# Threshold attention and a gated feed-forward layer on one core: the switch from the first to the second order of the work at slot 20 instead of slot 22

## The chip, the cores and the metric

The kernel runs on one core of one Trainium2 chip. The metric is the device time of one execution in microseconds (us). Engines are named as in the profile: PE (TensorE, matrix products and transposes), DVE (VectorE), ACT (ScalarE), POOL (GpSimd) and SP (SyncE, which here only issues DMAs). "PEld" is the loading of weights into PE.

## What is computed

Eight batches with eight heads, 576 tokens, head size 64. First an attention that keeps only scores near the row's maximum:

```python
scores = scale * np.matmul(q, k.transpose(0, 1, 3, 2))
thresh = np.max(scores, axis=-1, keepdims=True) - tau
scores = np.where(scores >= thresh, scores, -1000000000.0)
attn = softmax(scores)               # with 1e-09 added to the sum
x = np.matmul(attn, v)               # heads side by side: 4608 tokens x 512
```

Then a feed-forward layer on these 4608 tokens, with `w_in` of 512x2048 and `w_out` of 2048x512:

```python
h = x @ w_in
g = h * np.clip(h + 3.0, 0.0, 6.0) / 6.0
out = g @ w_out
```

## The kernel before, in words

**Slots.** Heads are taken four at a time (a quad, two pairs of heads; two quads make a batch, 16 quads in all). A quad has nine slots: four blocks of 128 query rows for each of its two pairs, and one slot (slot 8 of the quad) with the last 64 rows of all four heads. The 144 slots are walked by one hand-written loop. The program is not scheduled by a planner: each engine executes its instructions in the order in which the loop body emits them.

**One slot.** A slot `n` has these steps, for two heads at once:

- `scores` (L278): PE multiplies keys and queries in f32 into PSUM, 576 columns for each head.
- `sm_max` (L303): DVE copies the scores to SBUF and takes each row's maximum. `sm_bias` (L308): POOL makes the threshold from it.
- `sm_mask` (L312) and `sm_exp` (L317): ACT masks, then takes exponentials and their row sums.
- `sm_recip` (L320): DVE inverts the sums. `sm_norm` (L325): POOL scales the probabilities and writes them as bf16 (tile `pn`, four buffers).
- The probabilities are transposed for the product with the values. In most slots SP issues a DMA transpose (L333). In slots marked `on_chip` (L479: numbers below N1 - 1, in six of the nine places of a quad) PE does it with nine 128x128 transposes (L340) and DVE copies the result (L341).

**What stands beside the slots.** `av_main` and `av_rest` (L349, L352) multiply probabilities and values; `products` says after which slot. `turns` says in which slot a quad's queries and keys are transposed; in the first two batches PE does this (L233, L258, L260) and the results are copied out of PSUM by DVE, or, for the keys, by `copy_out` (L219), which picks DVE up to slot N1 and ACT afterwards.

**The feed-forward layer** is cut into items. One item of the first projection (`mm1`, L384) is eight 128x128 by 256 matmuls; ACT (even slots, L392) or DVE (odd slots, L394) computes relu(h + 3), and DVE multiplies it with h (`mm1_gate`, L407). An item's PSUM bank (HB) can be reused when its gate is done. The second projection (`mm2_part`, L418) is cut into parts of four 128x128 by 512 matmuls; four parts make a tile of 128 tokens, which DVE or ACT scales (L426, L424) and SP writes out (L439).
 
**Two orders.** Up to slot N1 - 1 the loop runs the first order: scores for slot n + 2 in every slot, exponentials one slot late, no feed-forward work. From slot N1 on it runs the second order: one first-projection item in each slot as long as `todo1` has one, two parts of the second projection (`second`, L520, `pieces`) in each even slot as long as `todo2` has some, and scores for the next two slots in one burst at the end of each odd slot. In the second order the scores of odd slots lie in other PSUM columns (`first`, L272) than those of even slots. If `pieces` is not zero, the item of the following odd slot cannot use bank OB, which holds the second projection's sum, and goes to HB. Up to slot N2 (28) ACT takes the exponentials of an even slot ahead of its relu, later behind it.

**DMAs.** SP loads queries and keys; POOL loads values, both weight matrices (with a cast to bf16, one or two pieces in a slot, the last pieces of `w_out` in slots 28 and 29) and, from quad 4 on, the last 64 rows of the keys (`rest`, L124).

**The end.** Behind the loop, `rest1` and `rest2` work off the remaining items. The last token tile is one sum of sixteen matmuls; `last_out` (L656) has ACT scale and write its left half and DVE its right half.

Of the kernel before, what the change touches and what calls it, by code (L numbers as in the profile page):

```python
# [9 lines left out]
F32 = mybir.dt.float32  # L10
# [3 lines left out]
Act = mybir.ActivationFunctionType  # L14

P = 128
# [4 lines left out]
def kernel(  # L21
# [10 lines left out]
    nc = tc.nc  # L32
    B, H, S, D = q.shape
    assert (B, H, S, D) == (8, 8, 576, 64)
    d_model, d_ff = moe_w_in.shape
    NPAIR = H // 2
    KI = d_model // P
    NI = d_ff // P
    NQUAD = B * H // 4
    NSLOT = 9  # L40
    NB = 2
    N0 = 3
    N1 = 22
    N2 = 28
    HB, OB = 6, 7
    scale = 1.0 / math.sqrt(D)
# [14 lines left out]
    o_pool = ctx.enter_context(tc.tile_pool(name="op", bufs=3))  # L61
# [5 lines left out]
    ps = ps_pool.tile([P, 8, 512], F32, name="ps")  # L67
# [15 lines left out]
    def load_quad(quad):  # L83
        b, g = divmod(quad, 2)
        nat[quad] = (nat_pool.tile([P, 1152], F32, tag="nq", name="nq"),
                     nat_pool.tile([P, 4, 4, D], F32, tag="km", name="km"),
                     nat_pool.tile([P, 2 * D], F32, tag="kr", name="kr"))
        nq, km, kr = nat[quad]

        def main(dst, src, h, order, by=nc.sync):  # L90
            by.dma_start(out=dst[:, :, h, :], in_=src[b, 4 * g + h, 0:512, :].rearrange(order, t=4))

        def blocks_q(n, a, j):
            c = 32 * (2 * a + j)
            nc.sync.dma_start(out=nq[c:c + 32, n * S:(n + 1) * S].rearrange("p (k d) -> p k d", d=32),
                              in_=q[b, 4 * g + 2 * n + a, :, 32 * j:32 * j + 32].rearrange("(k r) d -> r k d", r=32))

        def blocks_k(n, a, j):
            c = 32 * (2 * a + j)
            nc.sync.dma_start(  # L100
                out=km[c:c + 32].rearrange("p t h d -> p (t h d)")[:, n * 512:(n + 1) * 512].rearrange(
                    "p (t m d) -> p t m d", t=4, d=32),
                in_=k[b, 4 * g + 2 * n + a, 0:512, 32 * j:32 * j + 32].rearrange("(m r t) d -> r t m d", r=32, t=4))

        def load_k(n):
            if b < NB:
                for a in range(2):
                    main(km, k, 2 * n + a, "(p t) d -> p t d")
            else:
                for a in range(2):  # L110
                    for j in range(2):
                        blocks_k(n, a, j)

        def load_q(n):
            if b < NB:
                for a in range(2):
                    main(nq[:, 0:1024].rearrange("p (t h d) -> p t h d", h=4, t=4), q, 2 * n + a, "(t p) d -> p t d",
                         by=nc.scalar if quad == n == 0 else nc.sync)
            else:
                for a in range(2):  # L120
                    for j in range(2):
                        blocks_q(n, a, j)

        def rest():  # L124
            for dst, src in ((kr[:], k), (nq[:, 1024:1152], q))[0:2 if b < NB else 1]:
                for n in range(2):
                    (nc.sync if b < NB else nc.gpsimd).dma_start(out=dst[64 * n:64 * n + 64, :].rearrange("p (h d) -> p h d", h=2),
                                      in_=src[b, 4 * g + 2 * n:4 * g + 2 * n + 2, 512:S, :].rearrange("h p d -> p h d"))

        def both():  # L130
            rest()
            load_k(1)

        if b < NB:
            loads.extend((lambda: load_k(0), lambda: load_q(0), rest, lambda: load_k(1), lambda: load_q(1)))
        else:
            loads.extend((lambda: load_q(0), lambda: load_k(0), lambda: load_q(1), both))
# [22 lines left out]
    w_out_sb = singles.tile([P, NI, d_model], BF16)  # L160
# [34 lines left out]
    gbuf = g_pool.tile([P, NI, 2 * S], BF16, name="g")  # L195
# [21 lines left out]


    def copy_out(out, in_):  # L219
        if 0 <= now <= N1:  # L220
            nc.vector.tensor_copy(out=out, in_=in_)
        else:
            nc.scalar.copy(out=out, in_=in_)  # L223
# [46 lines left out]
        return evict  # L270

    def first(n):  # L272
        return n > N1 + 2 and n % 2

    def score_col(n, a):
        return (704 if first(n) else 128) + (0 if a else 1536)
# [137 lines left out]
    def mm2_part(bb, mt, part, ob=OB):  # L414
        if part == 0:
            o_ps[0] = ps[:, ob, :]
        for ni in range(part * 4, part * 4 + 4):
            nc.tensor.matmul(o_ps[0], gbuf[:, ni, mt * P:(mt + 1) * P], w_out_sb[:, ni, :],  # L418
                             start=(ni == 0), stop=(ni == NI - 1))
# [17 lines left out]
    def flush():  # L437
        for o, i in late:
            nc.sync.dma_start(out=i, in_=o)  # L439
        late.clear()  # L440
# [34 lines left out]
    for quad in range(NQUAD):  # L475
        for slot in range(NSLOT):
            sl = Slot()
            sl.quad, sl.slot, sl.n = quad, slot, len(queue)
            sl.on_chip = len(queue) < N1 - 1 and (slot in (1, 3, 5, 7, 8) or slot == 0 and quad > 0)  # L479
            queue.append(sl)  # L480
    scores(0)
    sm_max(queue[0])
    sm_bias(queue[0])
    scores(1)

    turns = {1: [("q", 1)], 2: [("k", 1)], 3: [("rest", 0)]}

    def turn_at(n, job, of):
        turns.setdefault(n, []).append((job, of))
# [10 lines left out]
    for quad in range(NQUAD):  # L500
        p0, p1 = 2 * quad, 2 * quad + 1
        if quad < NB:
            jobs = ((8, p0, 0, 512), (13 - 2 * quad, p1, 0, 512), (15 - 3 * quad, None, 0, 0))
        else:
            jobs = [(7 - quad % 2 + 2 * i, *of) for i, of in enumerate(
                ((p0, 0, 256), (p0, 256, 256), (p1, 0, 256), (p1, 256, 256), (None, 0, 0)))]
        for after, *of in jobs:
            products.setdefault(quad * NSLOT + after, []).append((quad, *of))
# [10 lines left out]

    def second():  # L520
        nonlocal pieces, bb, mt, part
        pieces = 2 if now % 2 == 0 and todo2 else 0
        for _ in range(pieces):
            bb, mt, part = todo2.pop(0)
            mm2_part(bb, mt, part)
# [127 lines left out]
    count = [1, 0 if todo2 and todo2[0][2] else 1]  # L653


    def last_out():  # L656
        osb = o_pool.tile([P, d_model], F32, tag="osb", name="osb")
        r0, c = B * S - 64 - P, d_model // 2
        nc.scalar.activation(out=osb[:, 0:c], in_=o_ps[0][:, 0:c], func=Act.Copy, scale=1.0 / 6.0)
        nc.scalar.dma_start(out=out[r0:r0 + P, 0:c], in_=osb[:, 0:c])  # L660
        nc.vector.tensor_scalar_mul(out=osb[:, c:2 * c], in0=o_ps[0][:, c:2 * c], scalar1=1.0 / 6.0)
        nc.sync.dma_start(out=out[r0:r0 + P, c:2 * c], in_=osb[:, c:2 * c])

    def rest1(item, then, on_act=True):
        h = mm1(item, hb=(0, 1, 3, 4)[count[0] % 4])
# [4 lines left out]
    def rest2():  # L670
        while todo2:
            bb, mt, part = todo2.pop(0)
            mm2_part(bb, mt, part, ob=OB - count[1] % 2)
            if part == 3:
                flush()
                if (bb, mt) == (B // 2 - 1, 8):
                    last_out()
                else:
                    late.extend(mm2_out(bb, mt, on_act=(count[1] % 2 == 0)))
                count[1] += 1  # L680

    av_main(2 * last + 1, 0, 256)()
# [50 lines left out]
```

## Time and profile before

| what | us |
|---|---|
| median of 7 runs (lowest to highest) | 516.6 (516.39 to 517.53) |
| the profiled execution | 516.39 |
| span of its trace | 514.6 |
| PE busy | 504.2 (98%) |
| ACT busy | 451.8 (88%) |
| DVE busy | 441.9 (86%) |
| POOL busy | 300.0 (58%) |

So 1.8 us of the profiled execution lie outside the span. The granted TensorE clock is 0.998 of full speed. "Busy" is to be read with care: the ends of pipelined matmuls are modelled, so PE counts as busy for part of the time in which it waits. Which engine sets the pace of a stage is read from the chain of waits and from the timeline, not from the shares alone.

### The profile page before, as it was taken

The numbers are of one execution on the slowest core, as the hardware profiler recorded it, in microseconds if no ns is written. First come the engines' busy times: TensorE is split into PE (matmuls) and PEld (weight loads), VectorE is DVE, ScalarE is ACT, GpSimd is POOL, SyncE is SP. The second block draws the span as 40 slices with busy tenths as digits, with TensorE's granted clock in tenths as the row PEclk, the third lists the DMA queues.
The fourth block names the chain that finished last, engine by engine and source line by source line (L and its number), as shares of the span: only waits on it lengthen the run. The fifth ranks groups of instructions, "written<-read, shape, count | busy, mean of one in ns | idle before, by whom it ended". The sixth has DMA issues, their size and how long they took to land.

```text
span 514.6 us, 12094 instructions
## 1 busy us (share of the span) xinstructions
PE 504.2 (98%) x4127; PEld 318.1 (62%) x4127; DVE 441.9 (86%) x1124; ACT 451.8 (88%) x980; POOL 300.0 (58%) x538
## 2 busy tenths in 40 slices
PE   8999999999999999999999999999999999999997
PEld 6655566666656666666656666666655666667563
DVE  3789898998999999999999999999999999887260
ACT  3999989999999999999999999999999999986060
POOL 1788888756666666666566756667566655552000
PEclk9999999999999999999999999999999999999999
DMA  6998999989999999999899999999999996655132
GB/s 140 176 165 144 155 149 173 166 150 193 163 167 162 177 178 150 181 170 171 162 182 152 187 165 164 169 159 175 156 172 174 182 177 115 113 103 89 74 63 61
DMA packets 314094, 78.77 MB, mean 153 GB/s; under 512 B 296624, under 2 KB 309168, under 8 KB 314032
## 3 DMA queue, kind: packets, MB, share of 16 engines
q1 hardware_dynamic: 294464, 67.90, 77.5%
q0 software_dynamic: 18368, 9.71, 15.3%
q8 instruction: 32, 0.52, 0.4%
q10 hardware_dynamic: 1200, 0.39, 0.3%
q14 instruction: 30, 0.25, 0.2%
HBM read 36.70 MB, written 9.44 MB: 90 GB/s over the span
## 4 chain that ended last, share of the span: by engine, by line
PE 79%; ACT 5%; DVE 2%; issue 0%
PE ps L288 24%; PE ps L418 24%; PE ps L384 20%; PE ps L349 7%; PE ps L379 3%; ACT s L317 2%; ACT s L312 2%; PE ps L352 1%; ACT r L392 1%; DVE g L407 1%; DVE r L394 0%; PE ps L340 0%; DVE s L303 0%; ACT kT L223 0%; PE ps L258 0%
## 5 line engine op out<-in xcount | busy, mean ns | idle before, releaser
L325 POOL TENSOR_SCALAR pn<-s,rinv 128x576 bf16<-128x576 f32 x288 | 211.4, 747 | 18.9 <-issue 4.8
L303 DVE TENSOR_SCALAR_CACHE_REDUCE s<-ps 128x576 f32<-128x576 f32 x288 | 205.0, 748 | 16.5 <-PE ps L288 8.3
L312 ACT ACTIVATE s<-s,bias 128x576 f32<-128x576 f32 x288 | 205.8, 763 | 5.1 <-POOL bias L308 4.7
L317 ACT ACTIVATE s<-s 128x576 f32<-128x576 f32 x288 | 192.5, 671 | 0.3
L288 PE MATMUL ps<-kT,qT 64*128 64x384 f32 (+7 forms) x1280 | 175.4, 419 | 3.9 <-DVE s L303 2.4
L288 PEld LDWEIGHTS ps<-kT,qT 64*128 64x128 f32 (+1 forms) x1280 | 102.9, 175 | 60.3 <-issue 15.8
L418 PE MATMUL ps<-w_out_sb,g 128*128 128x512 bf16 x576 | 134.1, 379 | 0.0
L384 PE MATMUL ps<-xT,w_in_sb 128*128 128x256 bf16 x1024 | 130.9, 273 | 0.8 <-DVE g L407 0.8
L384 PEld LDWEIGHTS <-w_in_sb 128*128 128x128 bf16 x1024 | 95.7, 98 | 40.6 <-issue 21.7
L308 POOL TENSOR_SCALAR bias<-m 128x2 f32<-128x2 f32 x144 | 27.1, 188 | 150.5 <-DVE rinv L320 133.8
L407 DVE SCALAR_TENSOR_TENSOR g<-r,ps 128x512 bf16<-128x512 f32 x128 | 87.8, 686 | 14.9 <-ACT r L392 11.0
L418 PEld LDWEIGHTS <-g 128*128 128x128 bf16 x576 | 56.2, 98 | 56.8 <-issue 0.4
L392 ACT ACTIVATE r<-ps,three 128x512 f32<-128x512 f32 x81 | 55.6, 687 | 24.7 <-PE ps L384 20.4
L317 ACT ACTIVATION_READ_ACCUMULATOR s<-s 128x1 f32 x288 | 54.6, 189 | 0.0
L394 DVE TENSOR_SCALAR r<-ps 128x512 f32<-128x512 f32 x63 | 42.8, 680 | 0.0
L349 PE MATMUL ps<-pT,vm 128*64 128x256 bf16 (+1 forms) x480 | 39.1, 285 | 0.0
L349 PEld LDWEIGHTS <-vm 128*64 128x64 bf16 x736 | 27.2, 110 | 16.1 <-issue 14.4
L360 DVE CAST xT<-ps 128x256 bf16<-128x256 f32 (+1 forms) x60 | 26.2, 436 | 10.2 <-PE ps L352 10.2
L426 DVE TENSOR_SCALAR osb<-ps 128x512 f32<-128x512 f32 x31 | 20.8, 673 | 8.4 <-PE ps L418 8.4
L303 DVE DVE_READ_ACCUMULATOR s<-ps 128x1 f32 x288 | 23.8, 83 | 0.0
L320 DVE RECIPROCAL rinv<-rsum 128x2 f32<-128x2 f32 x144 | 23.0, 160 | 0.6 <-ACT s L317 0.6
L144 POOL DMA_DIRECT2D vm<-in_v_dram x28 | 21.4, 766 | 0.7 <-issue 0.7
(57 smaller groups left out, 252.4 us busy)
## 6 DMA issues: line engine op xcount, KB each, us to landing
out_dram<-osb SPq DMA_DIRECT2D x31, 256.0 KB, 2.6
nq<-in_q_dram SPq DMA_DIRECT2D x96, 72.0 KB, 3.4
km<-in_k_dram SPq DMA_DIRECT2D x96, 64.0 KB, 3.2
vm<-in_v_dram POOLq DMA_DIRECT2D x24, 128.0 KB, 3.9
km<-in_k_dram SPq DMA_DIRECT2D x16, 128.0 KB, 3.8
w_in_sb<-in_moe_w_in_dram POOLq DMA_DIRECT2D x16, 128.0 KB, 3.7
w_out_sb<-in_moe_w_out_dram POOLq DMA_DIRECT2D x16, 128.0 KB, 3.7
pT<-pn SPq DMA_TRANSPOSE x117, 3.8
```

The source lines that it names most:

```text
L288: nc.tensor.matmul(ps_flat[rows, c0:c0 + w], qT_of(pair)[a * 64:(a + 1) * 64, q0:q0 + rows.stop - rows.start], kT_of(pair)[a * 64:(a + 1) ...
L303: nc.vector.tensor_scalar(out=sl.s[:, i, :], in0=ps_flat[:, c0:c0 + S], scalar1=1.0, scalar2=None, op0=Alu.mult, op1=Alu.max, accum_out=sl ...
L308: nc.gpsimd.tensor_scalar(out=sl.bias[:], in0=sl.m[:], scalar1=-scale, scalar2=tau, op0=Alu.mult, op1=Alu.add)
L312: nc.scalar.activation(out=s, in_=s, func=Act.Prelu, bias=sl.bias[:, i:i + 1], scale=scale, alpha=REJECT)
L317: nc.scalar.activation(out=s, in_=s, func=Act.Exp, accum_out=sl.rsum[:, i:i + 1])
L325: nc.gpsimd.tensor_scalar(out=pn[:, i, :], in0=sl.s[:, i, :], scalar1=sl.rinv[:, i:i + 1], scalar2=1.0, op0=Alu.mult, op1=Alu.mult)
L349: nc.tensor.matmul(pb[a * 64:(a + 1) * 64, :], vm[:, 2 * hp + a, c * D:(c + 1) * D], pT[:, 5 * a + c, cols], start=(c == 0), stop=False)
L384: nc.tensor.matmul(ps[:, hb, n * 256:(n + 1) * 256], w_in_sb[:, ki, (ni + n) * P:(ni + n + 1) * P], xT[b][:, ki, c0:c0 + 256], start=(ki = ...
L392: nc.scalar.activation(out=r, in_=hps, func=Act.Relu, bias=three[:])
L394: nc.vector.tensor_scalar(out=r, in0=hps, scalar1=3.0, scalar2=0.0, op0=Alu.add, op1=Alu.max)
L407: nc.vector.scalar_tensor_tensor(out=out, in0=r, scalar=6.0, in1=hps, op0=Alu.min, op1=Alu.mult)
L418: nc.tensor.matmul(o_ps[0], gbuf[:, ni, mt * P:(mt + 1) * P], w_out_sb[:, ni, :], start=(ni == 0), stop=(ni == NI - 1))
```

## The change

It has five parts.

1. `N1` is 20 instead of 22. The second order begins two slots earlier. With it, slots 17, 18 and 19 are no longer transposed by PE and DVE but by DMA (`N1 - 3` in place of `N1 - 1`), and `first` holds for slot 23 too.
2. The products of quad 1's second pair are taken in two column halves after slots 18 and 21, and its last rows after slot 23; before, the whole pair came after slot 20 and the last rows after slot 21. `second` gets a table: three parts in slot 36, one in each of slots 38, 42 and 44, otherwise two.
3. The last rows of quad 4's keys are loaded by SP instead of POOL.
4. `copy_out` uses DVE up to slot 23 (before: 22). The keys of pair 1 are transposed in slot 1 instead of slot 2.
5. The last token tile is multiplied in two column halves, in PSUM banks 2 and 5; DVE scales each, ACT's queue and SP write them.

```diff
-    N1 = 22
+    N1 = 20
...
-                    (nc.sync if b < NB else nc.gpsimd).dma_start(out=dst[64 * n:64 * n + 64, :].rearrange("p (h d) -> p h d", h=2),
+                    (nc.sync if quad < 5 else nc.gpsimd).dma_start(out=dst[64 * n:64 * n + 64, :].rearrange("p (h d) -> p h d", h=2),
...
     def copy_out(out, in_):
-        if 0 <= now <= N1:
+        if 0 <= now < N1 + 4:
...
     def first(n):
-        return n > N1 + 2 and n % 2
+        return n > N1 + 2 and n % 2 == 1
...
-            sl.on_chip = len(queue) < N1 - 1 and (slot in (1, 3, 5, 7, 8) or slot == 0 and quad > 0)
+            sl.on_chip = len(queue) < N1 - 3 and (slot in (1, 3, 5, 7, 8) or slot == 0 and quad > 0)
...
-    turns = {1: [("q", 1)], 2: [("k", 1)], 3: [("rest", 0)]}
+    turns = {1: [("q", 1), ("k", 1)], 3: [("rest", 0)]}
...
-            jobs = ((8, p0, 0, 512), (13 - 2 * quad, p1, 0, 512), (15 - 3 * quad, None, 0, 0))
+            jobs = (((8, p0, 0, 512), (9, p1, 0, 256), (12, p1, 256, 256), (14, None, 0, 0)) if quad else
+                    ((8, p0, 0, 512), (13, p1, 0, 512), (15, None, 0, 0)))
...
-        pieces = 2 if now % 2 == 0 and todo2 else 0
+        pieces = min(len(todo2), {36: 3, 38: 1, 42: 1, 44: 1}.get(now, 2)) if now % 2 == 0 else 0
...
-    def last_out():
-        osb = o_pool.tile([P, d_model], F32, tag="osb", name="osb")
+    def last_tile(mt):
         r0, c = B * S - 64 - P, d_model // 2
-        nc.scalar.activation(out=osb[:, 0:c], in_=o_ps[0][:, 0:c], func=Act.Copy, scale=1.0 / 6.0)
-        nc.scalar.dma_start(out=out[r0:r0 + P, 0:c], in_=osb[:, 0:c])
-        nc.vector.tensor_scalar_mul(out=osb[:, c:2 * c], in0=o_ps[0][:, c:2 * c], scalar1=1.0 / 6.0)
-        nc.sync.dma_start(out=out[r0:r0 + P, c:2 * c], in_=osb[:, c:2 * c])
+        for half, by in enumerate((nc.scalar, nc.sync)):
+            o_half, columns = ps[:, (2, 5)[half], 0:c], slice(half * c, half * c + c)
+            for ni in range(NI):
+                nc.tensor.matmul(o_half, gbuf[:, ni, mt * P:(mt + 1) * P], w_out_sb[:, ni, columns],
+                                 start=(ni == 0), stop=(ni == NI - 1))
+            osb = o_pool.tile([P, d_model], F32, tag="osb", name="osb")
+            nc.vector.tensor_scalar_mul(out=osb[:, 0:c], in0=o_half, scalar1=1.0 / 6.0)
+            by.dma_start(out=out[r0:r0 + P, columns], in_=osb[:, 0:c])
...
             bb, mt, part = todo2.pop(0)
+            if (bb, mt) == (B // 2 - 1, 8):
+                flush()
+                last_tile(mt)
+                todo2.clear()
+                continue
             mm2_part(bb, mt, part, ob=OB - count[1] % 2)
             if part == 3:
                 flush()
-                if (bb, mt) == (B // 2 - 1, 8):
-                    last_out()
-                else:
-                    late.extend(mm2_out(bb, mt, on_act=(count[1] % 2 == 0)))
+                late.extend(mm2_out(bb, mt, on_act=(count[1] % 2 == 0)))
```

## The prediction, as it was put on record

> **What bounds the kernel now.** I read the slices and the chain's shares first:
>
> ```profile
> PE   8999999999999999999999999999999999999997
> ...
> PE 79%; ACT 5%; DVE 2%; issue 0%
> ```
>
> PE is full in every slice, but ACT (88% of the span) and DVE (86%) nearly so, and the shares do not say which one sets the pace where. The chain of waits, in order of time, does:
>
> ```profile
> 90.16 1.34 ACT s L317 x4
> ...
> 110.99 0.98 PE ps L384 x8
> 111.97 1.73 PE ps L418 x8
> ```
>
> From 77.6 to about 104 us (slots 23 to 31) the chain runs through ACT's exponentials and masks; from about 106 us on it is PE alone, a pair of slots taking 6.38 to 6.5 us (first-projection item 0.98, two parts 1.73, item 0.98, values about 0.6, scores 2.14). So a slot moved ahead of 106 us competes with ACT and DVE, and work taken out behind it is worth PE time, down to what ACT needs for a pair: four exponentials and four masks at 0.67 and one relu of 0.69, 6.0.
>
> How full DVE is where the second order begins, I read from the busy time by stretches:
>
> ```profile
> core 0: us, PE busy (x) PEld busy (x) DVE busy (x) ACT busy (x) POOL busy (x), PEclk, DMA share, GB/s
> ...
> 66.43:92.72 26.29, 25.64 (x237) 17.23 (x234) 24.34 (x64) 24.46 (x55) 22.64 (x42) 1.00 1.04 162
> ```
>
> DVE idles 1.95 us and ACT 1.83 of 26.3. POOL's and PE's columns are no guide (PE's includes waiting).
>
> **What moves as a whole.** The order of the built instructions shows that behind slot 45 PE's sequence is the same in both kernels, the end included, but for the last tile. So no feed-forward work leaves the end: the items run out. The two items that move to slots 20 and 21 are missing from slots 36 and 37, and slot 28 gains two parts of the second projection and slot 36 one, taken from slots 38, 42 and 44, one from each. The account is therefore: what the early slots pay, against what slots 36 to 45 give back. PE's own work falls only by 27 transposes (9 take 0.55 from start to start of the next, 1.65 in all), in a stretch where PE is not the bound.
>
> **1. Keys of pair 1 in slot 1: -0.2.** In slot 2 PE waits 0.87 for DVE's copy of these keys (18.00 us), and ACT then 0.40 for a bias (21.13). With the copy (0.67) in slot 1 that wait goes, but four transposes (0.60) stand ahead of the scores of slot 3 and delay its mask by about 0.2. Ends: 0 to -0.4. The keys' DMA was issued by 6.1 us and lands 3.8 later by its group; it is needed at 14.
>
> **2. Slots 17 to 27.** On DVE three transposed copies (0.74) and a copy of 0.68 go: 2.9. Added are two gates (0.69), one relu (0.68), two half copies (0.42) and two key copies (0.28, from ACT): 3.5. DVE has 0.6 more to do, against 1.95 idle. On ACT a relu of 0.69 is added; two key copies (0.53) go, and two waits: 0.95 at 77.08 for the copy queued ahead on DVE, and 0.70 at 71.22, where the mask of slot 22 waits for a bias that POOL makes at 71.00, behind the issue of the last key rows (69.10 to 70.35) and of a weight piece. The kernel after takes that issue off POOL. So at slot 28 ACT is about 1.5 ahead by its own count and DVE 0.6 behind if none of its idle time is used. Each waits for the other, so I take 0.4 ahead: the maximum that starts at 91.40 (slot 29's) starts at 91.0. Ends: 0.6 behind, 1.5 ahead.
>
> SP's load: it gets three transposes (1.3 each) and two key loads (0.65 each), 5.2 us, behind blocks of four loads of 2.9 to 3.8. Counted on from 58.3, the transpose of slot 20 is issued at about 77.6 instead of 73.3 and, by its median landing of 3.8 (up to 5.6 in this stretch), lands at 82. The product that reads it is at 87.7 (slot 27), and the scaling that reuses its buffer at 83.6. It fits, with 1 to 2 us to spare. The product of slots 18 and 19 comes at 82 and its data at 77.
>
> **3. Slots 28 to 31: the new wait.** Slot 28 now has two parts, so slot 29's item goes to bank HB and waits for slot 28's gate. That gate is late, because up to slot 28 ACT's relu stands behind the exponentials:
>
> ```profile
> 90.84 1.92 PE L384 MATMUL ps<-xT,w_in_sb 128*128 128x256 bf16 x16
> ...
> 94.06 0.68 ACT L392 ACTIVATE r<-ps,three 128x512 f32<-128x512 f32 x1
> ...
> 94.77 0.69 DVE L407 SCALAR_TENSOR_TENSOR g<-r,ps 128x512 bf16<-128x512 f32 x1 [0.54 <-ACT r L392]
> ```
>
> Before, both items run in one go at 90.84, the parts of slot 30 first follow at 97.42, and the gate at 94.77 delays nobody. After: DVE does the maxima of slots 29 and 30 from 91.0 to 93.9, the gate to 94.55. PE, done with its parts at about 93.5, waits for it. Queued behind on PE are slot 29's item (to 95.6), the values (96.15), the scores of 32 and 31 (98.3), slot 30's item (99.25) and parts (101.0). DVE waits for these scores with the maximum of 31, ACT with slot 30's relu. On DVE: copy, relu, gate, key transpose (0.70), maximum to 100.0, gate of slot 30 to 100.8. PE goes on at 101.0: item, values 102.55, scores, and slot 32's item starts at 104.7. Before it starts at 103.85. **Cost of 2 and 3 together: +0.85.** Ends: +2.1 (DVE 0.6 behind, and gate and relu in series with the scores once more) and -1.0 (nothing waits).
>
> The last piece of `w_out` is issued by POOL at 97.20; the group's 3.7 puts it at 100.9. Slot 30's eighth matmul now reads it, at 99.25 + 7 x 0.216 = 100.8, so this wait is nothing as long as the one above stands; if the early slots go faster, it is what is late next.
>
> **4. Slots 36 to 45: -1.8.** Slots 36 and 37 lose two items (1.96) and gain a part (0.87): the pair of 6.49 becomes 5.40, above ACT's 5.33 without a relu: -1.09. In the pairs from 38, 42 and 44 a part of 0.87 goes, but it covers the way from item to gate:
>
> ```profile
> 343.95 1.05 PE L384 MATMUL ps<-xT,w_in_sb 128*128 128x256 bf16 x8
> ...
> 345.04 0.69 ACT L392 ACTIVATE r<-ps,three 128x512 f32<-128x512 f32 x1 [0.84 <-PE ps L384]
> ...
> 345.75 0.69 DVE L407 SCALAR_TENSOR_TENSOR g<-r,ps 128x512 bf16<-128x512 f32 x1
> ```
>
> The item ends at 344.93, the gate at 346.44, 1.51 later; the next item starts at 346.56. Two parts (1.73) fill that, one (0.87) leaves 0.64 of waiting. Each pair gains 0.23, three 0.69. Ends: -1.1 (the three give nothing) and -2.2 (they gain down to ACT's 6.0).
>
> **5. The last tile: -0.4.**
>
> ```profile
> 510.81 0.38 ACT L659 ACTIVATE osb<-ps 128x256 f32<-128x256 f32 x1 [2.86 <-PE ps L418]
> ...
> 511.23 0.42 DVE L661 TENSOR_SCALAR osb<-ps 128x256 f32<-128x256 f32 x1 [6.63 <-ACT osb L659]
> 511.68 0.34 SPq L662 DMA_DIRECT2D out_dram<-osb  x1
> ```
>
> DVE's half waits for ACT's half: from PE's end to the last issue 0.90. After, 0.04 + 0.42 + 0.03 remain: -0.41. The product in halves is 32 matmuls of 256 columns instead of 16 of 512: by the chain's rows 3.49 for 32 such (item rows at 491.70) against 10.37 / 48 x 16 = 3.46: +0.03. The last DMA is again 128 KB. Ends: -0.5 and, at the 0.122 of an isolated item's matmul (0.98 / 8), +0.03.
>
> Here a rule speaks against the change. The Trainium skill, page "TensorE: Matmul & The Clock Gate", section "Back-to-back issue gap", gives 81 ns for a sustained matmul of 128 columns with its weight load and 131 ns for one of 512, so that halving the columns would far from halve the time. An estimate from that page, 98 ns in between, makes the halves 3.13 against 2.10, and this step a loss of 0.6. The trace's 0.216 and 0.109 do not show such a floor at 256 columns, and I go by them.
>
> **Sum:** -0.2 + 0.85 - 1.78 - 0.38 = -1.51. Against the profiled execution (span 514.6 + 1.8 = 516.39): **514.9 us**. The median of the runs shown is 516.6, 0.2 higher.
>
> **Rivals.**
> A. The early slots come free: ACT is 1.5 ahead at slot 28 and most of the wait in 29 is absorbed. Then steps 2 and 3 cost between +0.2 and -1.0, and the time is 513.0 to 514.2. For it: DVE's 1.95 idle. Against it: the series of gate and scores above, and `w_out`'s last piece.
> B. The gain is used up: steps 2 and 3 cost 1.5 to 2.1, and at the upper end the thin pairs give only 1.1. That is -0.2 + 1.5 - 1.78 - 0.38 = -0.9 to -0.2 + 2.1 - 1.1 - 0.4 = +0.4, so 515.5 to 516.8. For it: DVE and PE then take turns. Against it: the idle time that DVE has now.
> C. Slower, by SP's queue: the DMA engines' share is 1.04 in 66 to 93 us. If the transpose of slot 20 lands later still than counted, POOL's scaling of slot 24 waits for its buffer, the maxima four slots on wait for theirs, and each further us goes into the time. With the slack of those buffers it decides from a landing behind about 85.5; at 89 it costs 3.5 against 1.5 won: 518.4. Landings of at most 5.6 speak against it.
>
> **How the numbers follow.** Forecast (514.2 to 515.5): 0.44. A: 0.24. B: 0.24. C: 0.08. The range leaves out C and the outer quarters of A and B, 0.2 in all: 513.3 to 516.4. About 0.2% (1.03 us) is what a measurement of this kernel can tell from no change. Faster by more are A and 0.40 of the forecast; within it are the other 0.04 and B; slower is C. So faster 0.64, within 0.2% 0.28, slower 0.08.
>
> **What would show it.** Right: in slot 29 PE's item waits for `DVE g L407` for about 1 us; slot 32's item starts 0.5 to 1 later than 103.85 (less 0.2); slot 46's about 1.1 earlier than 149.55; at the end no DVE wait for ACT, and the last issue about 0.5 us behind PE. Wrong: PE waiting for a DMA in slot 30 (`w_out`), POOL's scaling waiting for a DMA at 82 to 86 us, pairs of 6.4 in slots 38 to 45, or the last 32 matmuls taking over 3.6.

## The result, and the profile after

The kernel after takes 525.9 us (median of 16 runs, 519.09 to 529.37), the kernel before 516.65 (41 runs, 516.39 to 517.58). The ratio is 1.0138, 95% interval 1.0122 to 1.0153 (here and below ratios leave out the longest executions as disturbed, which the medians contain): **slower**, where 514.9 was predicted, and even the lowest time of after lies above each of these 41 times of before. The profiled execution of after is a long one, 529.37 (span 527.6); what it shows is compared below with shorter ones of its variants.

The page of after, with lines that answer to those of before (slices of PE, its granted clock, shares of the chain; last, the median landing of `w_out`'s pieces, that is the time from issue to arrival in us, 3.7 before):

```profile
PE   8999998669999999999999999999999999999997
...
PEclk9999999969999999999999999999999999999999
...
PE 78%; DMA 5%; DVE 3%; ACT 2%; POOL 1%; issue 0%; POOLq 0%; DVEq 0%
...
w_out_sb<-in_moe_w_out_dram POOLq DMA_DIRECT2D x16, 128.0 KB, 8.5
```

Nearly all of the loss lies in two slices of 13.2 us (92 to 119 us): from slot 28's first-projection item to slot 32's the trace takes 25.4 us, before 13.0, and the whole span is 13.0 longer. PE is no longer full there, its clock falls, and DMAs stand in the chain, where there were none. The chain of waits of after, in order of time (start, duration, what), names them:

```profile
79.69 6.04 DMA pT<-pn
...
85.91 0.76 POOL pn L325
...
90.06 11.77 DMA pT<-pn
...
102.00 1.41 POOL pn L325 x2
103.42 8.08 DMA w_out_sb<-in_moe_w_out_dram
...
112.34 1.71 PE ps L384 x8
...
117.97 0.98 PE ps L384 x8
```

The first link is slot 20's transpose: issued at 79.69, landed at 85.73, and POOL's scaling, which reuses its buffer, starts only then. Four slots later the same stands there again: slot 24's transpose takes 11.77, POOL's scaling of slot 28 waits for it until 102.00, and only behind that scaling does POOL issue the last piece of `w_out`. The last two lines are two items of the same size, 1.71 at 112 us and 0.98 at 118: it is the clock that differs.

So `w_out`'s last piece is late for two reasons. Its landing takes longer (8.08 against 3.6), and it is issued 6.2 us later than before, because POOL, which issues it, first has to wait for a buffer that a transpose still reads. POOL's timeline, after and then before:

```profile
102.00 1.47 POOL L325 TENSOR_SCALAR pn<-s,rinv 128x576 bf16<-128x576 f32 x2 [1.29 <-DMA pT<-pn]
103.42 0.58 POOL L169 DMA_DIRECT2D w_out_sb<-in_moe_w_out_dram  x1
```

```profile
97.20 0.57 POOL L169 DMA_DIRECT2D w_out_sb<-in_moe_w_out_dram  x1
```

The timeline of after for PE shows the predicted wait in slot 29 (first line) and then waits inside the second projection, of which two are printed:

```profile
96.94 1.03 PE L384 MATMUL ps<-xT,w_in_sb 128*128 128x256 bf16 x8 [1.68 <-DVE g L407]
...
105.98 0.46 PE L418 MATMUL ps<-w_out_sb,g 128*128 128x512 bf16 x1 [2.95 <-DMA w_out_sb<-in_moe_w_out_dram]
...
109.45 0.59 PE L418 MATMUL ps<-w_out_sb,g 128*128 128x512 bf16 x1 [1.70 <-DMA w_out_sb<-in_moe_w_out_dram]
```

They are four, 2.95, 0.73, 1.70 and 1.50: 6.9 us of waiting for single pieces of `w_out`, the last of which lands at 111.5 (before: 100.8). The busy time by stretches, after and then before (columns as in the prediction: busy us of PE, PEld, DVE, ACT, POOL, then the granted clock, the DMA engines' share, and GB/s):

```profile
84.00:90.00 6.00, 5.36 (x52) 3.78 (x48) 5.78 (x16) 6.00 (x14) 4.30 (x10) 1.00 1.28 141
...
102.00:108.00 6.00, 2.08 (x8) 0.59 (x6) 2.99 (x11) 3.64 (x8) 3.50 (x6) 0.85 1.36 113
108.00:114.00 6.00, 3.05 (x13) 1.49 (x12) 0.69 (x1) 1.59 (x5) 1.80 (x4) 0.50 1.23 198
```

```profile
84.00:90.00 6.00, 5.68 (x46) 3.83 (x46) 5.84 (x16) 6.00 (x14) 5.03 (x10) 1.00 1.13 184
```

In 84 to 90 us the DMA engines are busier than before (share 1.28 against 1.13) and move a quarter less, 141 against 184 GB/s. And in the last two stretches, 102 to 108 and 108 to 114 us, PE gets 0.85 and then 0.50 of its clock.

How the queue gets there can be read from the DMA part of both traces for 80 to 100 us (issues, KB each, median us to landing), before and then after:

```profile
w_out_sb<-in_moe_w_out_dram POOLq DMA_DIRECT2D x10, 128.0 KB, 3.7
pT<-pn SPq DMA_TRANSPOSE x6, 5.3
```

```profile
w_out_sb<-in_moe_w_out_dram POOLq DMA_DIRECT2D x11, 128.0 KB, 9.5
pT<-pn SPq DMA_TRANSPOSE x6, 10.6
```

The demand is the same, six transposes (and one of the last rows) and ten or eleven pieces, and landings take 2.0 and 2.6 times as long. In the trace of after the transposes issued at 79.69, 81.63, 83.28, 86.99, 90.06 and 93.26 land at 85.73, 89.51, 93.16, 98.27, 101.82 and 106.49, one in 3.5 to 5.1 us, while a slot wants one in about 3.0. The first three of them were issued within 3.6 us, because SP had come late out of two key-row loads and four key loads (75.52 to 79.59). In before, SP is through with its loads at 73.1; the three from slot 20 on are issued at 73.27, 75.15 and 78.81 and land in 4.0 to 5.9.

### The profile page after: what moved, and what is told of

Its sections match the earlier page's. It is cut to its first block, busy times and chain, and to the rows that moved or that the text cites. A ratio compares the mean times of both kernels' runs of the same rounds, so it can differ in the third digit from the quotient of the medians.

```text
span 527.6 us, 12086 instructions
## 1 busy us (share of the span) xinstructions
PE 507.0 (96%) x4126; PEld 320.6 (61%) x4126; DVE 441.5 (84%) x1125; ACT 451.4 (86%) x977; POOL 298.8 (57%) x536
## 4 chain that ended last, share of the span: by engine, by line
PE 78%; DMA 5%; DVE 3%; ACT 2%; POOL 1%; issue 0%; POOLq 0%; DVEq 0%
PE ps L288 24%; PE ps L418 22%; PE ps L384 20%; PE ps L349 7%; DMA pT<-pn 3%; PE ps L379 3%; DMA w_out_sb<-in_moe_w_out_dram 2%; PE ps L352 1%; DVE s L303 1%; DVE g L407 1%; ACT s L317 1%; PE ps L662 1%; ACT r L392 1%; ACT s L312 1%; POOL pn L325 1%; DVE r L394 0%
## 5 line engine op out<-in xcount | busy, mean ns | idle before, releaser
L288 PE MATMUL ps<-kT,qT 64*128 64x192 f32 (+7 forms) x1280 | 175.0, 420 | 2.3 <-DVE s L303 1.9
L418 PE MATMUL ps<-w_out_sb,g 128*128 128x512 bf16 x560 | 132.4, 380 | 6.9 <-DMA w_out_sb<-in_moe_w_out_dram 6.9
L418 PEld LDWEIGHTS <-g 128*128 128x128 bf16 x560 | 54.5, 98 | 61.5 <-issue 7.2
```

The lines of the kernel that those rows point to most:

```text
L288: nc.tensor.matmul(ps_flat[rows, c0:c0 + w], qT_of(pair)[a * 64:(a + 1) * 64, q0:q0 + rows.stop - rows.start], kT_of(pair)[a * 64:(a + 1) ...
```

## The experiments

Two theories stood against each other: that the loss is a **backlog of the DMA engines** (transposes and `w_out` pieces together) which the change tips over, and that the **order from slot 20** is itself the loss, whatever the DMAs do. All times were taken beside runs of the kernel before with medians of 516.7 to 516.9 (single times of before reach 519.4 in the set of e5 to e8, 518.0 in the others). "Landing" is the longest of a transpose issued in 66 to 112 us, and of a piece of `w_out`, in the profiled execution; "PE waits" is for DMAs, 60 to 140 us.

| run | us: median (lowest to highest) | ratio (95% interval) | landing, us | PE waits, us |
|---|---|---|---|---|
| before | 516.65 (516.39 to 517.58) | | 5.9 / 5.6 | 0 |
| after | 525.9 (519.09 to 529.37) | 1.0138 (1.0122 to 1.0153) | 13.2 / 11.8 | 7.2 |
| e1 | 525.83 (525.69 to 526.23) | 1.0176 (1.016 to 1.0191) | 5.8 / 5.9 | 0 |
| e13 | 518.42 (517.99 to 520.63) | 1.0033 (1.0018 to 1.0048) | 9.3 / 8.1 | 0 |
| e2 | 517.61 (516.24 to 520.74) | 1.0022 (1.0002 to 1.0041) | 8.2 / 6.9 | 0.6 |
| e10 | 516.88 (516.37 to 517.98) | 1.0004 (0.9995 to 1.0013) | 7.4 / 5.3 | 1.1 |
| e4 | 518.78 (517.18 to 525.4) | 1.0032 (1.0021 to 1.0042) | 10.0 / 8.0 | 3.4 |
| e6 | 518.64 (517.13 to 521.65) | 1.0026 (1.0009 to 1.0043) | 10.6 / 7.8 | 2.2 |
| e5 | 519.81 (517.41 to 527.47) | 1.0038 (1.0019 to 1.0057) | 7.8 / 6.9 | 0 |
| e12, e5 again | 522.09 (519.17 to 526.63) | 1.0107 (1.0057 to 1.0158) | 11.9 / 10.2 | 5.8 |
| e14 | 518.33 (517.0 to 519.36) | 1.0027 (1.0015 to 1.0038) | 7.1 / 6.4 | 0.9 |
| e3 | 520.65 (516.79 to 523.71) | 1.0067 (1.0036 to 1.0098) | 10.5 / 8.6 | 3.2 |
| e7 | 521.17 (520.4 to 522.49) | 1.0074 (1.0051 to 1.0098) | 11.2 / 9.5 | 4.5 |
| e9 | 524.36 (520.57 to 527.88) | 1.0142 (1.009 to 1.0195) | 12.8 / 10.8 | 7.4 |
| e8 | 515.59 (515.47 to 516.25) | 0.9969 (0.9958 to 0.9981) | 7.0 / 6.3 | 0 |
| e11 | 513.97 (513.83 to 515.01) | 0.9947 (0.9933 to 0.996) | 6.5 / 5.9 | 0 |
| e15 | 516.72 (514.51 to 517.71) | 0.9993 (0.9979 to 1.0008) | 7.2 / 5.8 | 1.6 |

### Taking the load off the queue: e1 and e13

e1 is after with slots 17 to 19 transposed by PE and DVE, as before:

```diff
-            sl.on_chip = len(queue) < N1 - 3 and (
+            sl.on_chip = len(queue) < N1 and (
```

> The kernel after, but slots 17, 18 and 19 are transposed by PE and DVE again, so that three DMA transposes go. Theory Q (queue): these three transposes fill the DMA queue ahead of the last pieces of w_out, so with them gone w_out lands about 4 us after its issue (kernel after: 8.5 in the median), PE waits for no DMA in slots 28 to 30, and the time falls to 514.5 to 517; the three transposes on PE and DVE cost up to 2 us of that. Theory N (early need): w_out is simply read two slots too early, and the queue is full anyway; then w_out lands about as late as in the kernel after, and the time stays above 519.

The landings are those of before again and no PE wait for a DMA is left, so the three transposes belong to the backlog. This is not shown cleanly, since e1 also issues the later transposes further apart (at 82.40, 87.19 and 91.24). The time did not fall to 514.5 to 517 as theory Q had it, for a reason of its own: these nine-fold transposes now stand in the second order. Waits of e1, 60 to 130 us (total, times, longest):

```profile
ACT r L392 <- PE ps L384: 12.1, 4, 8.9
...
PE ps L384 <- DVE pT L341: 3.2, 2, 2.4
```

ACT stands for 8.9 us in one piece behind an item that PE has behind the transposes. The run therefore says that these DMAs matter, and nothing on the price of the order. e13 does that: it loads only eight of `w_out`'s sixteen pieces and uses each twice (half of `w_out` is left out).

```diff
-        for ni in range(NI):
+        for ni in range(8):
...
-                             ... w_out_sb[:, ni, :],
+                             ... w_out_sb[:, ni % 8, :],
...
```

> The kernel after, but only the first eight of the sixteen pieces of w_out are loaded, and the second projection multiplies with each of them twice: half of w_out is left out of the computation, while every engine has the same instructions but for the eight DMAs that POOL no longer issues between slots 24 and 29. Theory Q (the loss is a backlog of the DMA engines between 80 and 112 us, and w_out's pieces are a part of that backlog as well as its first victims): no wait of PE for w_out, the transposes issued from 80 us on land in under 8 us instead of 9 to 13, the granted clock stays at 1.0, and what is left is the cost of the order at slot 20 without any wait, +0.5 to +1.0: 517.0 to 517.8. Theory W (the transposes are late by themselves, with or without w_out): they still land in 9 to 12 us, PE waits for pT instead, and the time is 519 to 523. Theory R (only the last pieces come too late for the second projection, the order itself is the gain that the prediction saw): 514.9 to 515.5.

518.42: no PE wait for a DMA, full clock, but landings up to 9.3, more than the backlog theory allowed. The DMA part of e13, again 80 to 100 us:

```profile
w_out_sb<-in_moe_w_out_dram POOLq DMA_DIRECT2D x4, 128.0 KB, 6.5
pT<-pn SPq DMA_TRANSPOSE x8, 5.7
```

The backlog builds up as in after (slot 22's transpose, issued at 83.24, lands at 92.50) and is gone as soon as the last piece, issued at 84.3, has landed at 92.4: the next transposes land at 93.38, 94.41 and 96.20, one in 0.9 to 1.8 us instead of one in 3.5 to 5.1. So the two kinds together are the load, and without the late pieces 7.5 of the 9.2 us between the medians are gone (by the ratios 5.4 of 7.1). What stays, 1.6, is put down to the order and some late transposes (POOL waits 2.2 for them).

### What tips the queue: e2, e10, e4, e6, e5, e12, e14

e2 adds the three DMA transposes to before; e10 adds the key rows by SP as well:

```diff
-            sl.on_chip = len(queue) < N1 - 1 and (
+            sl.on_chip = len(queue) < N1 - 5 and (
...
-                    (nc.sync if b < NB else nc.gpsimd).dma_start(
+                    (nc.sync if quad < 5 else nc.gpsimd).dma_start(
```

> The kernel before, but slots 17, 18 and 19 are transposed by DMA, as in the kernel after: three DMA transposes more, nothing else. Theory Q: the landings of w_out and of the transposes between 80 and 110 us grow to 8 us and more, POOL waits for its buffers, and the time rises by 1 to 8 us although PE and DVE have less to do; less than in the kernel after, since w_out is read two slots later. Theory N: the landings stay at 4 to 6 us and the time is 0 to 1 us lower.

> The kernel before with only the DMA side of the change: slots 17 to 19 transposed by DMA and quad 4's last key rows loaded by SP. Theory Q (the queue is filled by the DMAs, whatever the order of the rest): landings of 8 us and more at 80 to 105 us as in the kernel after, where e2 without the key rows had up to 8.2; 517 to 521. Rival O (it takes the earlier second order, which moves the transposes of slots 20 on closer together): landings like e2's, and the time like e2's 516.2 to 520.7.

In the old order the added DMAs cost 0.2 to 1.1 us by the ratios, with landings up to 8.2. That is what rival O expected of e10; theory Q's 517 to 521 was wrong. The added DMAs alone are not the cause: it takes the earlier order as well. e4 (after with the key rows by POOL again) takes two DMAs off SP, e6 (after with slot 17 on PE and DVE) takes one:

```diff
-                    (nc.sync if quad < 5 else nc.gpsimd).dma_start(
+                    (nc.sync if quad < 4 else nc.gpsimd).dma_start(
```

```diff
-            sl.on_chip = len(queue) < N1 - 3 and (
+            sl.on_chip = len(queue) < N1 - 2 and (
```

> The kernel after, but the last rows of quad 4's keys are loaded by POOL again. Theory Q with the three transposes as cause: the landings stay at 8 us and more, and the time stays within 519 to 529. If SP's load, with the bunching of the transposes of slots 20 to 22, is the cause, SP issues them up to 1.3 us earlier and the time falls by several us. Theory N: no change but for a bias that waits 0.7 us.

> The kernel after, but slot 17 is transposed by PE and DVE, in slot 19 and so still in the first order; two added DMA transposes instead of three. Theory Q: the backlog is smaller, the largest landing of w_out 5 to 9 us, the time 515 to 520, between the kernel after and one without a backlog. Rival S: between as well, so this run tells how much one transpose is worth. If the time stays at 522 to 529, neither holds.

Each brings 7 of the 9 us back (by the ratios 5.5 and 5.8 of 7.1), though neither empties the queue (landings 10.0 and 10.6): the last piece of `w_out` lands at 105.7 and 104.1 instead of 111.5, and that is enough for most of the waits. e5 leaves the number of DMAs and moves quad 4's key and query loads two slots ahead, away from the transposes of slots 20 to 22; e12 is the same program again:

```diff
-        for ahead in {0: (1, 2), 9: (3,), 16: (4,)}.get(n, ...
+        for ahead in {0: (1, 2), 9: (3,), 14: (4,)}.get(n, ...
-        elif n not in (4, 12, 15, 18, 21) and not 23 < n < 30 ...
+        elif n not in (4, 18, 21) and not 23 < n < 30 ...
```

> The kernel after, but quad 4's queries and keys are loaded in slots 14 to 17 instead of 16, 17, 19 and 20 (slots 12 and 15, which load nothing now, take their turn); every DMA stays, the three added transposes too. Theory Q (a backlog in the DMA queue, made by the three transposes on top of these block loads): the landings of w_out and the transposes at 80 to 105 us fall to 4 to 6 us, PE waits for no w_out piece for more than 0.5 us, and the time is 514.5 to 516.5. Rival S (the three transposes alone are too much, whatever stands beside them): the landings stay at 8 us and more and the time above 518.

> The kernel of e5 once more, since its times lie in three groups (517.4, about 519.6, about 527) and its profile was one of the first. Theory Q: a profile of a run of 519 and more shows landings of w_out or transposes over 8 us and PE waiting for them; a profile of 517.4 shows none. Rival: the groups come from something else (the granted clock, the start), and the landings are short in all.

The ten times of e5 fall into 517.41, five at 519.2 to 520.0 and four at 526.6 to 527.5; none lies in theory Q's 514.5 to 516.5. Both ends are profiled, the long one in e12 (on another chip, but the ten times of e5, which show both ends, come from one). The stretches of e5 (517.41), 84 to 90 us, and of e12 (526.63), there and at 108 to 114:

```profile
84.00:90.00 6.00, 5.36 (x50) 3.78 (x48) 5.58 (x16) 6.00 (x13) 5.45 (x11) 1.00 1.30 181
```

```profile
84.00:90.00 6.00, 5.36 (x48) 3.74 (x46) 5.57 (x16) 6.00 (x13) 5.45 (x11) 1.00 1.43 129
...
108.00:114.00 6.00, 6.00 (x30) 3.83 (x31) 2.94 (x5) 3.29 (x8) 0.00 (x0) 0.51 1.05 209
```

Up to 90 us the engines do the same at the same times: the transposes are issued at 77.36, 80.13 and 83.14 in e5 and at 77.53, 80.04 and 83.05 in e12. They land after 6.4, 7.8 and 6.6 us in the one and 6.5, 9.0 and 9.4 in the other. From there e5 recovers and e12 does not, and PE has lost half its clock by 108. So one and the same program falls to either side, with the same issues up to 90 us. The reading that fits this is a load so near what the engines can do that small differences decide, and that the change brings the kernel there. e14 joins the early loads with slot 17 on PE and DVE:

> The kernel after with quad 4's queries and keys loaded from slot 14 instead of 16, and slot 17 transposed by PE and DVE as before: two transposes by DMA are added instead of three, and the loads stand apart from them. Each alone left 518.6 and 517.4 to 526. If the queue is near its limit (theory Q), both together keep it short in most executions: landings under 8 us, no wait of PE for w_out over 0.5, 517.0 to 518.0, and a spread under 2 us. If the backlog comes from something that neither touches (theory W), executions over 519 stay as frequent as with the early loads alone.

518.33, landings up to 7.1 and no time over 519.4: a kernel of this order whose executions stay together, a little slower than theory Q's 517.0 to 518.0. It is still 1.5 us slower than before. In its profiled execution PE waits 0.9 for the last piece of `w_out` (issued at 98.2, landed at 103.3); the rest is put down to the order.

### Giving `w_out` more time: e3, e7, e9

e3 starts the second projection at slot 30 (with its table kept, so that one tile of 128 tokens isn't written out), e7 does so with two parts in every even slot, and e9 is e5 with `N2` at 26, so that slot 28's relu stands ahead of the exponentials:

```diff
-        pieces = min(len(todo2), {36: 3, 38: 1, 42: 1, 44: 1}.get(now, 2)) if now % 2 == 0 else 0
+        pieces = min(len(todo2), {36: 3, 38: 1, 42: 1, 44: 1}.get(now, 2)) if now % 2 == 0 and now >= 30 else 0
```

```diff
-        pieces = min(len(todo2), {36: 3, 38: 1, 42: 1, 44: 1}.get(now, 2)) if now % 2 == 0 else 0
+        pieces = 2 if now % 2 == 0 and todo2 and now >= 30 else 0
```

```diff
-    N2 = 28
+    N2 = 26
```

> The kernel after, but the second projection starts in slot 30 instead of 28, when it did in the kernel before. Theory N: the loss goes, 514 to 516.5. Theory Q: w_out and the transposes still land 8 to 13 us after their issue and POOL still waits for its buffers; PE's waits for w_out shrink but don't all go, since the last pieces land at about 109 to 111 us and slot 32 reads them at about 105; 517 to 521.

> The kernel after, but the second projection starts in slot 30 with two parts in each even slot, as in the kernel before, without the table for slots 36 to 44. Theory Q: the landings stay at 8 us and more (the queue is the same up to slot 28), but w_out is read two slots later, so PE's waits for it fall under 3 us in sum; 516 to 520. If the early start of the second projection were the whole cause: 514.5 to 516.

> The kernel of e5 (after, with quad 4's loads early), with N2 = 26: in slot 28 ACT takes the relu ahead of the exponentials. It tests the wait of slot 29's item for slot 28's gate by itself, in a profile without waits for DMAs. Theory G (that gate costs PE time): the item of slot 29 starts 0.6 to 1.4 us earlier than in e5, slot 32's item up to 1.3 us earlier, and the lowest times are 516.2 to 517.0 instead of 517.4. Rival: DVE is the bound there, the gate moves ahead of two maxima of 0.7 and delays them, and slot 32's item starts within 0.3 us of e5's.

A later start takes all but 0.4 of the wait for `w_out` away and leaves the wait for the transposes. The waits of e7, 60 to 130 us:

```profile
POOL pn L325 <- DMA pT<-pn: 6.0, 5, 1.8
...
PE ps L349 <- DMA pT<-pn: 4.1, 3, 3.2
```

So the early start of the second projection is a part of the price but not the cause: with it gone the medians of e3 and e7 are 5.2 and 4.7 lower than after's and still 3.9 and 4.3 above before (theory Q's ranges were 517 to 521 and 516 to 520), and `w_out` is only the first to feel the backlog. e9 shows its edit at work up to slot 30, whose item starts 1.2 earlier than e5's (at 98.64, less the 0.7 by which e9's first exponential comes later, against 99.15), and then falls into the backlog like e12 (7.4 of PE waits). Whether it would pay without one stays open.

### The parts of the change without its order: e8, e11, e15

e8 is before with the keys of pair 1 in slot 1 and the last tile in halves. e11 adds the key rows by SP and one more slot of copies by DVE (`now < N1 + 2`, with N1 = 22). e15 adds the three DMA transposes to that: all of the change but the order.

> The kernel before with two parts of the change alone: the keys of pair 1 transposed in slot 1, and the last token tile in two halves. By the prediction's terms 0.2 and 0.4 less, 515.8 to 516.4; the trace of the kernel after shows 0.5 for the first and 0.2 for the second, 515.7 to 516.2. Both theories agree here; the run tells whether these two parts are worth their terms.

> The kernel of e8 (before, with the early keys and the last tile in halves), and of the change also the key rows by SP and copy_out by DVE for one slot more, without the order at slot 20 and without added transposes. If the waits that these two were to take away (0.70 and 0.95 us of ACT at 71 and 77 us) lie on the path: 514.4 to 515.4. If DVE or SP takes their place: 515.4 to 516.

> The kernel before with the keys of pair 1 in slot 1, the key rows of quad 4 by SP, the copies out of PSUM by DVE a slot longer and the last tile in halves (513.97), and with slots 17, 18 and 19 transposed by DMA as in the kernel after: all of the change but the order. If the order is what is paid for (theory O), the three transposes take 2.9 us off DVE where it is short and add at most a landing or two: 513.2 to 514.5. If the transposes by DMA fill the queue in any order that is this far ahead (theory W), the slots before the second projection have lost their slack and the time is 516 to 519.

**e11 is faster than both kernels: 513.97, ratio 0.9947 (0.9933 to 0.996).** Its 1.6 less than e8 go for the larger part with the two waits of ACT that the prediction named under step 2 (0.95 at 77.08, 0.70 at 71.22): one is gone, the other shorter. ACT's waits in 66 to 93 us, e8 and then e11:

```profile
ACT kT L223 <- DVE qT L266: 1.0, 1, 1.0
ACT s L312 <- POOL bias L308: 0.9, 2, 0.7
```

```profile
ACT r L392 <- PE ps L384: 0.5, 1, 0.5
ACT s L312 <- POOL bias L308: 0.4, 2, 0.3
```

e15 loses that again in seven of ten executions (516.6 to 517.7; the other three 514.5 to 514.9), although it takes 2.2 us of copies off DVE; its profiled execution is one of the short ones, so where the others lose it isn't shown. That is three times theory O's case or near it and seven times theory W's.

The lowest times make a ladder: before 516.4, e8 515.5, e11 513.8, with the transposes (e15) 514.5, with the order and the early loads (e5) 517.4. The order with the early loads costs 2.9 there, without a wait of PE for a DMA.

## Why the prediction was wrong, point by point

**The step that failed first is SP's and the DMA engines' load in step 2: "It fits, with 1 to 2 us to spare".** Slot 20's transpose was to be issued at 77.6 and to land at 82; it was issued at 79.69 and landed at 85.73. The term "three transposes (1.3 each)" was too small by 1.8 of these 2.1: their issues held SP for 2.48, 1.28 and 1.98.

```profile
66.72 2.48 SPq L333 DMA_TRANSPOSE pR<-pn  x1
69.38 1.28 SPq L333 DMA_TRANSPOSE pT<-pn  x1
...
73.49 1.98 SPq L333 DMA_TRANSPOSE pT<-pn  x1
```

The next two transposes followed within 3.6 us, and landings grew to 13.2 where I had taken 3.8 "(up to 5.6 in this stretch)". That reading was itself a little low: the transpose that before issues at 78.81 lands after 5.9. I took landings as a property of the operation. Here they depend on what else is in the queue, from 3.2 to 13.2 us for transposes of one size. A hint stood in the prediction, a DMA share of 1.04, which I had used for rival C only. It is no more than a hint: e11 has a share of 1.14 in 66.0 to 92.3 us, its landings stay at 6.5 or less, and its times stay within 1.2 us.

**Step 3's "this wait is nothing" for `w_out`** failed with it: 6.9 us in PE, and behind that the clock (next section). From slot 28's item to slot 32's the profiled execution takes 25.4 us (92.48 to 117.90); e5, with the same instructions in these slots, takes 14.1.

**Rival C** had the right queue and the right wait: it decides "from a landing behind about 85.5", the landing came at 85.73, and POOL's scaling starts at 85.91 in the chain. That its point fits so closely is in part luck, since POOL loses only 0.55 there, and in e13 the same transpose lands at 85.64 and the run loses 1.6 us. Its price was wrong (3.5). I let each late landing cost its own delay; but here the next ones grew (6.0, 7.9, 9.9, 11.3, 11.8 and 13.2 us), and the largest price is paid by PE for `w_out`, whose last pieces POOL issues late because it waits for its buffers. The chance of 0.08 rested on landings measured in before.

**Steps 2 and 3 without any backlog: +2.2 instead of +0.85.** The profiled execution of e5, in which PE waits for no DMA, shows them (start, duration, operation, wait):

```profile
73.94 0.76 DVE L303 TENSOR_SCALAR_CACHE_REDUCE s<-ps 128x576 f32<-128x576 f32 x1 [0.88 <-PE ps L288]
...
91.89 0.72 DVE L303 TENSOR_SCALAR_CACHE_REDUCE s<-ps 128x576 f32<-128x576 f32 x1
...
95.37 1.03 PE L384 MATMUL ps<-xT,w_in_sb 128*128 128x256 bf16 x8 [1.03 <-DVE g L407]
```

The new wait in slot 29 is there and of the predicted size, 1.03. What is wrong is where the slot begins: its maximum starts at 91.89, not at 91.0, though the early slots had won 0.5. "ACT is about 1.5 ahead by its own count" was a count of work. In e5 ACT waits 0.99 for an item (74.84) and DVE 0.88 for scores (73.94): so the first slots of the second order run at least in part in series, and the two engines do not use the idle time that they have. Slot 32's item starts at 105.64, 1.7 later than before (both counted from the first exponential), and 0.5 of gain is in that. The upper end, +2.1, was the right value.

**Step 4: -1.2 instead of -1.78.** From slot 32's item to slot 46 e5 takes 44.42, before 45.63. Slots 36 and 37 gave 0.9 (5.60 instead of 6.49), near the 1.09. The thin pairs gave 0.00 to 0.07 each, not 0.23: the pairs from 38, 42 and 44 take 6.32, 6.49 and 6.31 against 6.39, 6.49 and 6.38 before. That is the lower end, "the three give nothing". With both, the terms of rival B hold for the order by itself, at their upper end; e5's time of 517.41 lies above B's 516.8 all the same, by the 0.35 at the end (below) and some more.

**Step 5: right.** The end of after:

```profile
524.07 0.42 DVE L665 TENSOR_SCALAR osb<-ps 128x256 f32<-128x256 f32 x1 [1.32 <-PE ps L662]
524.52 0.34 SPq L666 DMA_DIRECT2D out_dram<-osb  x1
```

No wait for ACT is left; the last issue is 0.48 behind PE's end (524.04), and the 32 matmuls take 3.66 from the first start to the modelled end. The 3.49 of the prediction is from start to start of what follows; by the modelled end before's 32 item matmuls at 491.54 take 3.66 too, so the sign "over 3.6" was badly put, and halves of 256 columns cost no more than predicted. In e8 the way from PE's end to the end of the span is 3.38 instead of 3.81: -0.43 for -0.38.

**Step 1: the sign right, the size beyond its end.** The exponentials of slot 6 start 0.53 earlier, counted from those of slot 0 (e5: 16.15, before: 16.68); -0.2, at most -0.4, was predicted.

**One thing was not seen:** in all kernels of the new order that were compared, PE ends 0.35 later, counted from the last pair of exponentials (45.99 us after its start in e5, 45.63 in e8). In e5 a gate near the end waits for a buffer that a DMA still reads, and in e8 it does not:

```profile
498.52 1.28 DVE L407 SCALAR_TENSOR_TENSOR go<-r,ps 128x512 bf16<-128x512 f32 x2 [1.30 <-DMA g<-go]
```

"Behind slot 45 PE's sequence is the same" was true, and did not cover SP's. That this wait makes the 0.35 is argued, and what delays that DMA was not tried.

**What stays open:** why the DMA engines, with the same issues, move 181 GB/s in one execution and 129 in the next. The traces show where the rate is lost: transposes (queue q1) are fast alone and slow beside pieces of `w_out` (q0). By queue (packets, MB, share of the engines' time), 88.0 to 88.5 us of before, where the transposes are nearly alone, and then 96 to 98 us of after:

```profile
q1 hardware_dynamic: 563, 0.14, 127.2%
q0 software_dynamic: 2, 0.00, 0.4%
```

```profile
q1 hardware_dynamic: 656, 0.17, 114.9%
q0 software_dynamic: 60, 0.05, 16.1%
```

That is 0.28 MB of transposes in a microsecond against 0.085, while their packets hold the engines for about as large a share of the time. So each packet takes longer; the engines are not only fuller. What makes the packets slow is not shown.

## What to carry to other kernels

A landing time read from a profile holds for the load at which it was read. Here, with a DMA share of 1.0 to 1.4, transposes that were added and moved together with others landed one in 3.5 to 5.1 us where a slot wanted one in 3.0, and what was due behind them, on the other queue too, was late with them. Before a stage is started earlier, list what its first consumers read, which engine issues it and what that engine may wait for, and when the last load of it lands, and give that slack. Idle time of two engines at the start of a new order was no reserve here, where they hand the same tile back and forth; and a change in five parts is worth taking apart, since here three small parts (3, 4 and 5) carry all of the gain.

## What the runs showed of the hardware that was not expected

**The queue holds SP too.** As landings grow, the issue of a transpose itself takes longer. SP's timeline, after and then before (the same slot's transpose):

```profile
97.96 3.84 SPq L333 DMA_TRANSPOSE pR<-pn  x1
```

```profile
91.60 1.24 SPq L333 DMA_TRANSPOSE pR<-pn  x1
```

Transposes of SP and pieces of POOL slow down together, 5.3 to 10.6 and 3.7 to 9.5 us. The Trainium skill, page "DMA: Bandwidth & Descriptors", section "Queues, rings and completion order", says that each DMA engine takes turns between the queue rows it has work for; the landings agree, in that neither queue is spared.

**A PE that waits for DMAs pays twice.** An item takes 1.71 instead of 0.98 even when its data are there, because the granted clock has halved. Finer stretches of after show when:

```profile
106.00:106.14 0.14, 0.14 (x1) 0.08 (x1) 0.00 (x0) 0.00 (x0) 0.00 (x0) 1.00 1.62 84
106.16:116.38 10.22, 6.30 (x27) 3.13 (x27) 1.74 (x4) 3.29 (x8) 3.13 (x5) 0.50 1.20 182
116.40:120.00 3.60, 3.60 (x28) 2.29 (x25) 3.14 (x8) 1.02 (x2) 0.28 (x2) 1.00 0.69 152
```

The clock falls at 106.15, right behind the first of PE's four waits (2.95 us, up to 105.98), and stays at half for 10.2 us, in which the other three lie. The Trainium skill, page "TensorE: Matmul & The Clock Gate", section "Part 1: The HAM clock gate (the "warmup" mystery)", gives half the clock after an idle window of about 3.4 us. The 0.50 agrees; the length of a single wait does not tell it here. In e3 one of 1.82 is followed by half the clock:

```profile
95.20 0.63 PE L349 MATMUL ps<-pT,vm 128*64 128x256 bf16 x8 [1.82 <-DMA pT<-pn]
```

```profile
96.32:99.70 3.38, 3.38 (x17) 2.06 (x14) 1.99 (x4) 2.65 (x6) 1.41 (x4) 0.50 1.40 143
```

In after the wait of 1.68 at 96.94, for a gate, is not followed by it: the stretch 96 to 102 us has a clock of 1.00.
